# A top-k attention and quick-GELU kernel: from slot 25 on, all TensorE products as 64x64 quarters, in two halves across two PSUM banks, with units and loads in another order

## The chip, the cores and the metric

The kernel runs on one core of a Trainium2 chip. The metric is the device time of one execution in microseconds (us). The time of the kernel before is the median of three runs. One further execution was taken by the hardware profiler, and the profile and the trace come from it.

Engines are named as in the profile: PE (TensorE, the products), PEld (its weight loads), DVE (VectorE), ACT (ScalarE), POOL (GpSimd), SP (SyncE, which issues the DMAs).

## The reference

```python
# attention: q, k, v are (8, 8, 576, 64) float32; top_k = 32
scores = scale * np.matmul(q, k.transpose(0, 1, 3, 2))
kth = np.partition(scores, -top_k, axis=-1)[..., -top_k:-top_k + 1]
scores = np.where(scores >= kth, scores, -1000000000.0)
scores = scores - np.max(scores, axis=-1, keepdims=True)
attn = np.exp(scores)
attn = attn / (np.sum(attn, axis=-1, keepdims=True) + 1e-09)
attn_out = np.matmul(attn, v)                      # (B, H, S, D)
# bridge: x is (B*S, H*D) = (4608, 512)
h = x @ w_in                                       # w_in (512, 2048)
g = h * (1.0 / (1.0 + np.exp(-1.702 * h)))
return g @ w_out                                   # w_out (2048, 512)
```

Each row of scores keeps its 32 largest entries; the softmax over them weighs v. The result, heads side by side, goes through two matrix products with a quick GELU between them. All is float32.

## The kernel before, in words

**Slots.** The attention is cut into 144 slots, 18 for each of 8 batches (`slots`, from line 424). A slot is 128 query rows of two heads; the last 64 rows of a sequence (576 = 4 x 128 + 64) of two pairs of heads share a slot. For slot n:

- `scores(n)` (line 442) makes the scores on PE as 64x64 quarters into `score_banks` (tile s_ps); `copy_scores` (457) brings them to SBUF on ACT (sc).
- `pair_up` (466) makes the maximum and minimum of the two halves of a row on DVE; `topk` (486) finds the 32 largest by four rounds of MAX8 with MATCH_REPLACE8 between (tiles ranked and top). `find` (1172) runs slot m's rounds, with `pair_up(m + 1)` and `invert(m - 1)` (545: POOL some, DVE rden) among them.
- `bounds` (511) computes the threshold on POOL (cut, low); `mask` (526) and `exps` (534) make the masked exponentials on ACT (pr, den); `normalize` (559) scales them on POOL.
- `split` (595) copies pr apart in 16-bit halves on ACT (sc<-pr) and SP writes them to DRAM (rows); `turn_by_dma` (603) reads them back transposed (pt<-rows).
- `values_of_two` (675) multiplies two slots at once with v into two PSUM tiles (o): for the sequence's last 64 keys with v_e as quarters, for the others with v_l as 128x64 products (all 128 rows, half of the columns). `x_of_two` (703) copies them to xT on ACT.

**Blocks and units.** When all heads of 128 rows are there, they are a block (line 740). A block has four units of four pieces of 128 of the 2048 inner columns. For a unit: `hidden` (760) makes x @ w_in on PE (tile ph, 32 matmuls of 128x64, in one of the two buffers of `ps_t`, which o uses as well); `tanh` (782) takes tanh and a copy on ACT; `gate` (794) and `combine` (811) work on POOL and make the seven sums of a Strassen scheme on 2x2 blocks; `project` (864) multiplies them with w_out or its prepared sums into two PSUM banks (po0, po1; 28 matmuls of 128x64: seven products, two inner pieces, two column halves). After a block's fourth unit `leave_parts` (900) brings both banks to SBUF on ACT (raws<-po), POOL adds the products up (`merging`, by `merge_some`), and SP writes the rows out.

**Order.** Engines run their instructions in the order in which the kernel issues them. Up to slot 24 calls are collected and issued in a written-out order (ORDER, `issue_in_order`, 1358). From slot `COLLECTED` = 25 on `steady_pair(n)` (1281) issues two slots at a time. On PE a pair is: a projection, a hidden unit, s_ps of slot n+2, a hidden unit, a projection, s_ps of slot n+3, the values of slots n-3 and n-2. Behind the slots `last_units` (1347) finishes what is left. Every call passes through one recorder (line 131), so the profile has L131 for nearly all (L133 for what was collected).

**Loads.** `at(slot, ...)` (942) notes what falls due at a slot; `dues` (1150) hands it out. q and k of two heads are loaded (`load_both`, 371), split on ACT (`prepare_by_dma`, 375: halves), written to DRAM (qk_rows) and read back transposed (`turn` in it: qk_t<-qk_rows). FETCH (950) and READY (948) give the slots, relative to the batch's first, of the load and of the split.

## Time and profile before

| | |
|---|---|
| median of three runs | 1366.73 us |
| lowest and highest | 1366.28 and 1373.02 us |
| profiled execution: time | 1371.88 us |
| profiled execution: span of the program | 1370.1 us |
| granted TensorE clock, mean | 0.995 |
| DMA queue of the program | 526544 packets, 243.16 MB, 72.9% of 16 engines' span |
| PE instructions (products) | 22532, and as many weight loads |

How to read the profile's lines: a group line names the line of the kernel, engine and operation, then the tile written <- the tiles read, the shape, and xcount; behind it stand busy microseconds, the mean nanoseconds of one, and the engine's idle time before them with what ended it. The rows of the windows view give, for a stretch, each engine's busy time with its count of instructions, the granted clock, the DMA share and GB/s. The timeline merges like instructions that follow each other: start, time from the first start to the last end, what. Products of the code in float32 stand as two instructions each.

### The profile page before, as it was taken

To read this page: it belongs to the slowest core of one execution; us is meant where nothing else is said; L and a number is where in the kernel's file an instruction comes from. 1 tells how busy PE (TensorE), PEld (TensorE's weight loads), DVE (VectorE), ACT (ScalarE), POOL (GpSimd) and SP (SyncE) were. 2 spreads that over 40 slices of the span, in tenths; PEclk is the share of its full clock that TensorE was granted. 3 is DMA by queue.
4 is the path that set the end of the run, shared out by engine and by line. 5 is a ranking of instruction groups with operands and counts; after the bars stand their busy time and mean duration, and the time that the engine had idled before them with its cause. 6 is when DMAs were issued, how large, how long until landed. Compare 5 with 4: busy or idle time off the path is not lost.

```text
span 1370.1 us, 54342 instructions
## 1 busy us (share of the span) xinstructions
PE 1340.9 (98%) x22532; PEld 1202.3 (88%) x22532; DVE 1274.6 (93%) x3374; ACT 1166.2 (85%) x1936; POOL 978.4 (71%) x1782
## 2 busy tenths in 40 slices
PE   7899999999999999999999999999999999999998
PEld 5687588999989998999999999999998999999998
DVE  7999999999999999999999999999999999999912
ACT  6999898998889979898889888998988888888841
POOL 3888887777767776777777777777777777777770
PEclk9899999999999999999999999999999999999999
DMA  8443759677998767988899796988899767765540
GB/s 233 144 146 110 177 155 212 170 191 195 217 211 212 183 150 203 209 200 197 206 208 206 181 195 164 237 192 196 204 202 202 192 172 181 186 148 135 143 122 17
DMA packets 527223, 246.92 MB, mean 180 GB/s; under 512 B 458880, under 2 KB 505472, under 8 KB 526976
## 3 DMA queue, kind: packets, MB, share of 16 engines
q1 hardware_dynamic: 526544, 243.16, 72.9%
q8 instruction: 177, 2.90, 0.9%
q14 instruction: 70, 0.57, 0.1%
q10 hardware_dynamic: 432, 0.30, 0.1%
HBM read 46.01 MB, written 103.42 MB: 109 GB/s over the span
## 4 chain that ended last, share of the span: by engine, by line
PE 86%; DMA 4%; DVE 3%; ACT 3%; POOL 1%; SPq 1%; issue 1%; DVEq 0%; ACTq 0%; POOLq 0%
PE ph L131 31%; PE po L131 28%; PE o L131 10%; PE s_ps L131 9%; PE po L133 4%; DMA pt<-rows 2%; DVE ranked L133 2%; PE o L133 1%; DVE top L133 1%; PE s_ps L133 1%; SPq L131 1%; PE ph L133 1%; PE tp L133 1%; ACT sc L133 1%; DMA rows<-sc 1%
## 5 line engine op out<-in xcount | busy, mean ns | idle before, releaser
L131 DVE MAX8 top<-ranked 128x8 f32<-128x288 f32 (+1 forms) x952 | 526.7, 595 | 0.0
L131 PE MATMUL ph<-xT,win 128*64 128x128 f32 x8064 | 464.2, 273 | 0.0
L131 PEld LDWEIGHTS ph<-xT,win 128*64 128x64 f32 x8064 | 441.2, 137 | 25.9 <-issue 21.9
L131 DVE MATCH_REPLACE8 ranked<-top,ranked 128x288 f32<-128x288 f32 x714 | 382.0, 543 | 0.0
L131 ACT COPY sc<-pr 128x2304 uint16<-128x2304 uint16 x120 | 253.7, 2114 | 87.0 <-POOL pr L131 87.0
L131 POOL TENSOR_SCALAR pr<-pr,rden 128x576 f32<-128x576 f32 x240 | 177.3, 749 | 40.0 <-DVE rden L131 40.0
L131 PE MATMUL po<-wout,h 128*64 128x128 f32 x2000 | 194.2, 273 | 0.0
L131 PE MATMUL po<-raws,h 128*64 128x128 f32 x2000 | 194.2, 273 | 0.0
L131 ACT ACTIVATE pr<-sc,low 128x576 f32<-128x576 f32 x240 | 183.4, 770 | 0.2 <-POOL raws L131 0.2
L131 POOL TENSOR_SCALAR some<-den 128x2 f32<-128x2 f32 x120 | 26.7, 222 | 209.8 <-ACT pr L131 209.8
L131 ACT ACTIVATE sc<-sc,cut 128x576 f32<-128x576 f32 x240 | 174.1, 781 | 0.1
L131 DVE TENSOR_TENSOR ranked<-s_ps,sc 128x576 f32<-128x576 f32 x236 | 166.6, 747 | 4.3 <-ACT sc L131 4.3
L131 POOL TENSOR_TENSOR th<-th,h 128x512 f32<-128x512 f32 x123 | 157.7, 1282 | 10.3
L131 PE MATMUL po<-wout,th 128*64 128x128 f32 x2064 | 156.6, 273 | 0.0
L131 ACT COPY sc<-s_ps 128x576 f32<-128x576 f32 x234 | 138.0, 642 | 19.8 <-PE s_ps L131 9.7
L131 PE MATMUL s_ps<-qk_t 64*64 64x288 f32 x1872 | 140.5, 415 | 0.0
L131 PEld LDWEIGHTS po<-wout,h 128*64 128x64 f32 x2000 | 126.4, 137 | 0.0
L131 PEld LDWEIGHTS po<-raws,h 128*64 128x64 f32 x2000 | 126.4, 137 | 0.0
L131 PEld LDWEIGHTS po<-wout,th 128*64 128x64 f32 x2064 | 121.3, 137 | 0.0
L131 PE MATMUL o<-pt,v_l 128*64 128x128 f32 (+1 forms) x2144 | 120.7, 266 | 0.0
L131 PEld LDWEIGHTS o<-pt,v_l 128*64 128x64 f32 x2144 | 106.6, 137 | 9.9 <-issue 9.1
L131 POOL TENSOR_TENSOR h<-th 128x128 f32<-128x128 f32 x248 | 114.1, 460 | 0.3
(121 smaller groups left out, 2216.6 us busy)
## 6 DMA issues: line engine op xcount, KB each, us to landing
rows<-sc SPq DMA_DIRECT2D x134, 576.0 KB, 3.8
qk_rows<-halves SPq DMA_DIRECT2D x24, 576.0 KB, 5.2
out_dram<-raws SPq DMA_DIRECT2D x68, 128.0 KB, 3.6
raws<-in_moe_w_in_dram SPq DMA_DIRECT2D x16, 512.0 KB, 4.7
raws<-in_moe_w_out_dram SPq DMA_DIRECT2D x16, 512.0 KB, 3.7
qk_l<-in_q_dram SPq DMA_DIRECT2D x28, 256.0 KB, 4.2
qk_l<-in_k_dram SPq DMA_DIRECT2D x28, 256.0 KB, 4.4
v_l<-in_v_dram SPq DMA_DIRECT2D x4, 1024.0 KB, 7.5
```

The lines of the kernel that those rows point to most:

```text
L131: do(*args, **kwargs)
L133: self.engines.collected.append(lambda: do(*args, **kwargs))
```

## The change

From slot 25 on `quarter_pair` takes the place of `steady_pair`:

- Hidden units, projections and values are made of 64x64 quarters: 64 of the 128 rows of the contraction and 64 columns. Two units (or the two banks of a projection, or the two slots of the values) are made together. In a first half each quarter of the two PSUM banks takes one half of the rows (for hidden units and projections: rows 0 to 63 into one bank, rows 64 to 127 into the other); in the second half they change over, and a semaphore (`turned_over`), raised by the first half's last product, is waited for by the second half's first. The number of multiplications stays; the seventh product of the projection (s4 with b22) is split over both banks, so that 512 instead of 384 columns leave the second bank, and one more addition merges them.
- On PE a pair becomes: first half of two hidden units, first half of a projection, s_ps of slot n+2, second half of the hidden units, second half of that projection, first half of the next projection, s_ps of slot n+3, first half of the values, 8 matmuls of the projection's second half, second half of the values, the rest of the projection. At slot 25 one more projection is issued. `last_units` keeps its form for hidden units; its projections are in quarters where their block began so.
- Loads, splits and transposed reads of q and k move to other slots from the third pair of heads of batch 2 on.

```diff
...
@@ -225,7 +225,8 @@
     score_banks = pool("ps_s", 1, space=PSUM).tile([P, 2, 2, 512], F32, name="s_ps")
     ps_t = pool("ps_t", 2, space=PSUM)
     ps_p = pool("ps_p", 1, space=PSUM)
-    both_banks = [ps_p.tile([P, 512], F32, name=f"po{i}") for i in range(2)]
+    two_banks = lambda: [ps_p.tile([P, 512], F32, name=f"po{i}") for i in range(2)]
+    both_banks = two_banks()
     ident = const.tile([P, P], F32, name="ident")
     make_identity(tc.nc, ident[:])
@@ -397,6 +398,8 @@
         if b % 2 and hp > 1:
             at(b * PER + TURN, turn)
+        elif (b, hp) > (2, 1):
+            at(b * PER + READY[b % 2][hp] + 1, turn)
         else:
             turns.append(turn)
@@ -700,11 +703,76 @@
                 stop=(s, j) not in halves[k + 1 :],
             )
+    on_rows = lambda i: slice(i * TAIL, (i + 1) * TAIL)
+    turned_over = tc.alloc_semaphore("turned_over")
+    counted = [0]
+    def in_two_parts(homes, parts):
+        number = []
+        def part(n, first=0, last=None):
+            if n and not first:
+                nc.tensor.wait_ge(turned_over, number[0])
+            for home, at_, left, right, start, stop in parts[n][first:last]:
+                nc.tensor.matmul(homes[home][at_], lhsT=left, rhs=right, start=start, stop=stop)
+            if not n:
+                nc.tensor.drain(fusable=True).then_inc(turned_over, 1)
+                counted[0] += 1
+                number.append(counted[0])
+        return [lambda *some, n=n: part(n, *some) for n in range(2)]
+    two_turns = lambda: [ps_t.tile([P, 512], F32, name="tp") for _ in range(2)]
+    def values_in_quarters(held):
...
+        firsts, seconds = [], []
+        for k in range(0, len(of[0][1]), 2):
+            for o, ends, mains in of:
+                for r, j, cols, left, right in ends[k : k + 2]:
+                    firsts.append((o, j, r, cols, left, right))
+        own = {}
+        for o, j, r, *rest in firsts:
+            own[o, j] = r
+        for part, turned in ((firsts, 0), (seconds, 1)):
+            for k in range(len(of[0][2])):
+                for o, ends, mains in of:
+                    for j, cols, left, right in mains[k]:
+                        part.append((o, j, own[o, j] ^ turned, cols, left, right))
+        order = firsts + seconds
+        whose = [(o, j) for o, j, *rest in order]
+        steps = [
+            (
+                o, (on_rows(j), cols), left[on_rows(r)], right[on_rows(r)],
+                whose[k] not in whose[:k], whose[k] not in whose[k + 1 :],
+            )
+            for k, (o, j, r, cols, left, right) in enumerate(order)
+        ]
+        return homes, in_two_parts(homes, (steps[: len(firsts)], steps[len(firsts) :]))
     def x_of_two(held, o):
         for m, part in zip(held, o):
             b, t, hps = slots[m]
             x = xs[:, place_of(b, t), :, :]
+            part = part[:, 0:P]
             if t < NF:
                 nc.scalar.copy(out=x[:, hps[0], :], in_=part)
             else:
@@ -749,6 +817,7 @@
             if not self.whole:
                 self.left = [h * (FC // 2) + 2 * u + c for u in range(4) for h in range(2) for c in range(2)]
             self.done = 0
+            self.quarters = False
     ready = []
     to_gate, gated, to_project = [], [], []
@@ -779,6 +848,47 @@
         if not x.left:
             free.append(ready.pop(0).place)
+    quadrants = lambda a, b: ((a, 0, 0), (b, 1, 1), (a, 0, 1), (b, 1, 0))
+    def hidden_two():
+        if sum(len(x.left) for x in ready) < 2 * G:
+            return [lambda: hidden(ps_t), lambda: None]
+        units, homes = [], two_turns()
+        for _ in range(2):
+            x = ready[0]
+            fs, x.left = x.left[:G], x.left[G:]
+            units.append((fs, x))
+            if not x.left:
+                free.append(ready.pop(0).place)
+        parts = []
+        for turned in range(2):
+            part = []
+            for i in range(G):
+                for c in range(CC):
+                    for u, r, y in quadrants(turned, 1 - turned):
+                        fs, x = units[u]
+                        f = fs[i] * P + y * TAIL
+                        part.append(
+                            (
+                                u,
+                                (on_rows(y), slice(i * P, (i + 1) * P)),
+                                win[on_rows(r), c, f : f + TAIL],
+                                xs[on_rows(r), x.place, c, :],
+                                not turned and i == 0 and c == 0,
+                                turned == 1 and i == G - 1 and c == CC - 1,
+                            )
+                        )
+            parts.append(part)
+        first, second = in_two_parts(homes, parts)
+        def last():
+            second()
+            for ph, (fs, x) in zip(homes, units):
+                to_gate.append((ph[:], fs, x))
+        return first, last
     def tanh(aside):
         if to_gate:
@@ -861,8 +971,88 @@
         for _ in range(min(count, len(summing))):
             summing.pop(0)()
+    def leave_parts_of(x):
+        def leave_parts():
...
+            if x.quarters:
+                merging.append(add(o[:, 3, :], o[:, 3, :], o[:, 7, :]))
...
+    turned_last = [1]
+    def project_in_quarters():
+        if not to_project:
+            return [lambda: None, lambda *some: None]
+        x = to_project[0][3]
+        if not x.done:
+            x.quarters = True
+        if not x.quarters:
+            return [lambda: project(True), lambda *some: None]
+        g, sums, fs, x = to_project.pop(0)
+        a11, a12, a22, s1, s2, s3, s4 = sums
+        banks = (
+            ((1, a11, "b11"), (2, a12, "b21"), (0, s2, "t2"), (3, s4, "b22")),
+            ((0, a22, "t4"), (1, s1, "t1"), (2, s3, "t3"), (3, s4, "b22")),
+        )
+        parts = []
+        way = turned_last[0], 1 - turned_last[0]
+        for n, turned in enumerate(way):
+            part = []
+            for i in range(2):
+                for k in range(3 if turned else 4):
+                    for bank, r, y in quadrants(turned, 1 - turned):
+                        to, a, w = banks[bank][k]
+                        part.append(
+                            (
+                                bank,
+                                (on_rows(y), slice(to * P, (to + 1) * P)),
+                                a[on_rows(r), i, :],
+                                weight(w, fs[i])[on_rows(r), y, :],
+                                x.done == 0 and n == 0 and i == 0 and k == 0,
+                                x.done == FC - G and n == 1 and i == 1 and k == (2 if turned else 3),
+                            )
+                        )
+            parts.append(part)
+        turned_last[0] = way[1]
+        x.done += G
+        last = x.done == FC
+        first, second = in_two_parts(both_banks, parts)
+        def finish(*some):
+            second(*some)
+            if last and len(some) < 2:
+                leaving.append(leave_parts_of(x))
+        return first, finish
     def project(put_off_leaving=False):
+        if to_project[0][3].quarters:
+            for part in project_in_quarters():
+                part()
+            return leave_all()
         g, sums, fs, x = to_project.pop(0)
         if x.whole:
             for i, f in enumerate(fs):
@@ -897,30 +1087,8 @@
             for i in range(2):
                 nc.sync.dma_start(x.rows[:, i, :], ob[i * TAIL : (i + 1) * TAIL, :])
...
         if x.done == FC:
-            leaving.append(leave if x.whole else leave_parts)
+            leaving.append(leave if x.whole else leave_parts_of(x))
         if not put_off_leaving:
             leave_all()
@@ -947,7 +1115,6 @@
     READY = (-15, -11, -7, -3), (-17, -13, -9, -5)
     TURN = -3
-    FETCH = (-19, -13, -9, -5), (-19, -15, -11, -7)
     FETCH_1 = (-11, -6, -5, -4)
     VALUES = {(0, 1): 0, (2, 3): 2}, {(0, 1, 2, 3): 2}
     by_slot = dict(enumerate([2, 3, 3, 3, 3, 3, 3, 3, 3, 3, 3]))
@@ -966,9 +1133,12 @@
     for b in range(1, B):
         for hp in range(NP):
             if b > 1:
-                at(b * PER + FETCH[b % 2][hp], load_both, b, hp)
+                if (b, hp) < (2, 2):
+                    at(b * PER + (-19, -13)[hp], load_both, b, hp)
+                else:
+                    at(b * PER + READY[b % 2][hp] - 4, load_both, b, hp)
                 if (b, hp) != (2, 0):
-                    at(b * PER + READY[b % 2][hp], prepare_by_dma, b, hp)
+                    at(b * PER + READY[b % 2][hp] - 2 * ((b, hp) > (2, 1)), prepare_by_dma, b, hp)
             else:
                 at(b * PER + FETCH_1[hp], load_both, b, hp)
         for hps, n in VALUES[b % 2].items():
@@ -1344,6 +1514,79 @@
         if live(n + 1):
             bounds(n + 1)
+    def quarter_pair(n):
+        begin, prepare_some = dues(n)
+        if live(n - 1):
+            exponentials(n - 1)
+        combine()
+        merge_some(6 if n == COLLECTED + 2 else 3)
+        units = hidden_two()
+        units[0]()
+        leave_all()
+        first = project_in_quarters()
+        if n > COLLECTED:
+            first[0]()
+        prepare_some()
+        find(n, 8)
+        if live(n + 2):
+            scores(n + 2)
+        if n == COLLECTED:
+            first[0]()
+        units[1]()
+        first[1]()
+        if live(n - 1):
+            normalize(n - 1)
+            split(n - 1)
+        write_all()
+        gate()
+        begin(0)
+        if live(n - 1):
+            turn_by_dma(n - 1)
+        if live(n + 2):
+            copy_scores(n + 2)
+        if live(n):
+            bounds(n)
+        combine()
+        merge_some(4)
+        if live(n):
+            mask(n)
+            exps(n)
+        if n == COLLECTED:
+            leave_all()
+        tanh(True)
+        tanh(True)
+        prepare_some()
+        second = project_in_quarters()
+        second[0]()
+        find(n + 1, 8)
+        if live(n + 3):
+            scores(n + 3)
+        held = [m for m in (n - 3, n - 2) if live(m)]
+        o, values = values_in_quarters(held)
+        values[0]()
+        second[1](0, 8)
+        values[1]()
+        second[1](8)
+        if n == COLLECTED:
+            for part in project_in_quarters():
+                part()
+        if live(n):
+            normalize(n)
+            split(n)
+        write_all()
+        while turns:
+            turns.pop(0)()
+        begin(1)
+        if live(n):
+            turn_by_dma(n)
+        gate()
+        if live(n + 3):
+            copy_scores(n + 3)
+        x_of_two(held, o)
+        if live(n + 1):
+            bounds(n + 1)
     def last_units():
         hidden(ps_t)
@@ -1378,7 +1621,7 @@
             steady_pair(n)
         issue_in_order()
         for n in range(COLLECTED, N + 2, 2):
-            steady_pair(n)
+            quarter_pair(n)
         combine()
         while ready or to_gate or gated or to_combine or to_project:
             last_units()
```

More of the change, by code (lines that the diff above doesn't have):

```diff
@@ L130, in step @@
             if self.engines.collected is None:
-                do(*args, **kwargs)
+                return do(*args, **kwargs)
             else:
@@ L862, in sum_weights, with bring_out @@
             summing.pop(0)()
+    def leave_parts_of(x):
+        def leave_parts():
+            o = raws[:, 3, :].bitcast(F32).rearrange("p (r k) -> p r k", r=8)
+            for bank, count in enumerate((4, 4 if x.quarters else 3)):
+                nc.scalar.mul(
+                    out=o[:, 4 * bank : 4 * bank + count, :].rearrange("p r k -> p (r k)"),
+                    in_=both_banks[bank][:, 0 : count * P], mul=0.5 / RAISE**2,
+                )
+            add = lambda to, x, y: lambda engine: engine.tensor_tensor(out=to, in0=x, in1=y, op=ALU.add)
+            twice = lambda x: x.to_broadcast([P, 2, P])
+            merging.append(add(o[:, 0:3:2, :], o[:, 0:3:2, :], twice(o[:, 1:2, :])))
+            if x.quarters:
+                merging.append(add(o[:, 3, :], o[:, 3, :], o[:, 7, :]))
+            for to, by in ((6, 0), (0, 5), (3, 0)):
+                merging.append(add(o[:, to, :], o[:, to, :], o[:, by, :]))
+            merging.append(add(o[:, 4:6, :], o[:, 4:6, :], twice(o[:, 6:7, :])))
+            merging.append(lambda engine: writes.append(lambda: bring_out(o)))
+        def bring_out(o):
+            for y in range(2):
+                nc.sync.dma_start(
+                    x.rows[:, :, y * 2 * P : (y + 1) * 2 * P],
+                    o[y * TAIL : (y + 1) * TAIL, 2:6, :].rearrange("r (i h) k -> r i (h k)", i=2),
+                )
+        return leave_parts
@@ new lines @@
+    turned_last = [1]
[17 more added lines that the diff above has]
+            part = []
+            for i in range(2):
+                for k in range(3 if turned else 4):
[9 more added lines that the diff above has]
+                                x.done == FC - G and n == 1 and i == 1 and k == (2 if turned else 3),
+                            )
+                        )
+            parts.append(part)
[8 more added lines that the diff above has]
+        return first, finish
```

34 lines of the change are left out of this document (14 added, 20 removed).

## The prediction

> **What bounds the kernel now.** I read the page first, then the whole stretch that the change touches, then one pair of slots engine by engine.
>
> ```profile
> span 1370.1 us, 54342 instructions
> PE 1340.9 (98%) x22532; PEld 1202.3 (88%) x22532; DVE 1274.6 (93%) x3374; ACT 1166.2 (85%) x1936; POOL 978.4 (71%) x1782
> PE 86%; DMA 4%; DVE 3%; ACT 3%; POOL 1%; SPq 1%; issue 1%; DVEq 0%; ACTq 0%; POOLq 0%
> ```
>
> The chain that ended last is 86% TensorE. But the average hides a second engine. The reciprocal of a slot's denominators (tile rden) runs once in each slot, so its first and last start mark slots 25 to 143, and the windows view gives the busy time between them and in the tail behind them:
>
> ```profile
> L131 DVE RECIPROCAL rden<-some x119: 140/166/167, 265.2 to 1308.8; 128x2 f32<-128x2 f32 x119
> ```
>
> ```profile
> 265.00:1309.00 1044.00, 1040.85 (x18627) 953.61 (x18625) 1019.93 (x2698) 920.91 (x1494) 757.10 (x1446) 1.00 0.80 190
> 1309.00:1370.00 61.00, 55.15 (x1008) 54.22 (x1004) 9.45 (x25) 12.26 (x22) 21.74 (x36) 0.99 0.20 49
> ```
>
> Columns after the stretch and its length: PE, PEld, DVE, ACT, POOL. In the stretch with the slots PE idles 3.2 us and VectorE idles 24.1 us of 1044. VectorE's work is not changed, so **however much PE gets faster, this stretch cannot lose more than about 24 us**. The tail is PE alone.
>
> One pair of slots on PE (timeline; start, duration). Each float32 matmul of the code stands twice in the profile, so a hidden unit of 32 matmuls is x64; the po rows between the two shown run on to 711.69, and those between 714.84 and 717.90 are the second projection:
>
> ```profile
> 700.27 3.66 PE L131 MATMUL ph<-xT,win 128*64 128x128 f32 x64
> 703.86 1.20 PE L131 MATMUL s_ps<-qk_t 64*64 64x288 f32 x16
> 704.99 3.71 PE L131 MATMUL ph<-xT,win 128*64 128x128 f32 x64
> 708.54 0.61 PE L131 MATMUL po<-wout,th 128*64 128x128 f32 x8
> ...
> 711.69 1.20 PE L131 MATMUL s_ps<-qk_t 64*64 64x288 f32 x16
> 712.71 0.40 PE L131 MATMUL o<-pt,v_e 64*64 64x128 f32 x8
> 713.04 1.97 PE L131 MATMUL o<-pt,v_l 128*64 128x128 f32 x32
> 714.84 0.61 PE L131 MATMUL po<-wout,th 128*64 128x128 f32 x8
> ...
> 717.90 3.66 PE L131 MATMUL ph<-xT,win 128*64 128x128 f32 x64
> ```
>
> The pair takes 717.90 - 700.27 = **17.63 us on PE**. VectorE in the same time (timeline; the row of x4 at 711.71 holds the last two maxima of one slot and the first two of the next, so a slot goes from one such place to the next):
>
> ```profile
> 707.55 1.41 DVE L131 TENSOR_TENSOR ranked<-s_ps,sc 128x576 f32<-128x576 f32 x2
> 709.55 0.15 DVE L131 RECIPROCAL rden<-some 128x2 f32<-128x2 f32 x1
> 716.18 1.41 DVE L131 TENSOR_TENSOR ranked<-s_ps,sc 128x576 f32<-128x576 f32 x2
> 718.95 0.17 DVE L131 RECIPROCAL rden<-some 128x2 f32<-128x2 f32 x1 [0.69 <-POOL some L131]
> ```
>
> 716.18 - 707.55 = 8.63 us without a gap, so **17.26 us a pair is VectorE's floor**, 0.37 us under PE's 17.63. The next reciprocal comes 9.40 after the last one and shows who loses that time: PE is late with s_ps and the values, so ScalarE is late with its exponentials, GpSimd with "some", and VectorE waits.
>
> **The change, part by part.**
>
> *The form of the products.* A 128x64 product that used all rows becomes two of 64 rows, four of which run together. What one step costs is read from the rows above, with the length of one product:
>
> ```profile
> L131 PE MATMUL ph<-xT,win 128*64 128x128 f32 x8064 | 464.2, 273 | 0.0
> ```
>
> ```profile
> L131 PE MATMUL o<-pt,v_e x520: 216/269/320, 268.4 to 1295.9; 64*64 64x128 f32 x142, 64*64 64x64 f32 x32
> ```
>
> Old form: 64 instructions in 3.66, the last alone 0.27, so 31 steps of two in 3.39, **0.109 a step of two**. New form: v_e already has it (64*64, 128 columns, two PSUM tiles). Two steps of four take 0.40, less the last product 0.27, so 0.13 holds one step and the stagger of its four starts: 0.13 is the upper bound. s_ps, in the same form with 288 columns, makes four steps in 712.71 - 711.69 = 1.02, which is 0.113 for 128 columns with the entry. No row shows a reason for less than the old 0.109. I take **0.1095 a step of four**, the old one's, to which s_ps without its entry is nearest. Two products of the old form equal four quarters, so by themselves the products gain and lose nothing. What goes is the change of form around s_ps and v_e:
>
> - 703.86 to 704.99 is 1.13 for s_ps, where the second s_ps (v_e behind it in the same form) takes 1.02;
> - first hidden unit 3.59, second 3.55, against 32 steps x 0.109 = 3.49;
> - first projection 3.15 against 28 x 0.109 = 3.05; values 714.84 - 712.71 = 2.13 against 2 x 0.11 + 16 x 0.109 = 1.96.
>
> New pair: 64 + 56 + 18 = 138 steps x 0.1095 = 15.11, and two s_ps at 1.0, so **17.1 us against 17.63: 0.53 a pair less on PE**. That is below VectorE's 17.26, so the pair goes to 17.3. (The count of changes of form in the two programs' order: 250 before, 18 after, so the change does what it says.)
>
> *The semaphore between the halves.* Its increment rides on the last product of a first half. Waiting at the second half holds up everything behind it on PE. For hidden units and the first projection of a pair, between halves lie a projection part and s_ps (over 2 us); for the values only 8 matmuls, 4 x 0.11 = 0.44. The last product's result is there 0.27 after its start, 0.16 after its step: between 0 and 0.1, I take 0. In the tail two projections run their halves back to back: about 0.3 each.
>
> *Order on PE.* Both hidden first halves now follow the values closely: behind the last value product stand 16 matmuls of the projection (0.88) and then a step that needs both xT copies.
>
> ```profile
> 714.25 1.18 ACT L131 COPY sc<-s_ps 128x576 f32<-128x576 f32 x2 [0.84 <-PE o L131]
> 715.32 0.45 ACT L131 COPY xT<-o 128x128 f32<-128x128 f32 x2
> 715.63 1.47 ACT L131 ACTIVATE sc<-sc,cut 128x576 f32<-128x576 f32 x2
> 718.40 0.21 ACT L131 ACTIVATION_READ_ACCUMULATOR pr<-sc,low 128x1 f32 x1
> 718.50 0.98 ACT L131 ACTIVATE raws<-po 128x512 f32<-128x512 f32 x2
> ```
>
> Result 0.16 + copies 0.45 + two semaphores (0.1 each is my estimate) = 0.8 against 0.88: hidden, with nothing to spare. Every second pair a block's sums leave PSUM (raws<-po), which ScalarE does behind the exponentials: 719.48 - 715.63 = 3.85 after the masks begin, plus 0.1 for 128 more columns. Before, the next block's first projection came 8 us later; now it comes 3.5 (the hidden halves) after the projection's end. Values' end + 0.16 + 0.45 + 3.95 + 0.1 = 4.7 against 0.88 + 3.5 = 4.4: 0.3 in every second pair, up to 1 when the masks wait for VectorE. Bounds 0 to 0.5 a pair; I take 0.15, because PE then has 0.16 to spare against VectorE and a late PE hurts only past the reciprocal's slack. (Above, masks began at 715.63 and cost 0.77 there, so 714.86 would have cost none.) The one more GpSimd addition per block (about 0.46) lies in its idle time ("some" waits 207 us for ScalarE in this stretch, below).
>
> *Loads and transposes moved.* From batch 2 on q/k loads and their splitting come two slots earlier (one load in eight stays), and the transposing read comes three slots after the split instead of in the same pair of slots (the last two of odd batches stay). SyncE issues the same DMAs; they only move past rows/pt issues. Waits in the stretch:
>
> ```profile
> POOL some L131 <- ACT pr L131: 207.2, 119, 4.4
> DVE rden L131 <- POOL some L131: 18.6, 35, 3.7
> ACT xT L131 <- PE o L131: 15.3, 45, 0.5
> ACT sc L131 <- DMA rows<-sc: 6.7, 3, 3.9
> DVE ranked L131 <- ACT sc L131: 3.4, 3, 2.2
> PE o L131 <- DMA pt<-rows: 1.6, 2, 1.3
> ```
>
> DMA shows in few long waits (6.7 + 1.6 = 8.3 us in 5 places). I put that much of VectorE's 24.1 to DMA and leave it standing: bounds from all gone (-8) to doubled (+8).
>
> *The sum.* Stretch: 24.1 - 8.3 = 16 us of VectorE's idle time goes. This agrees with 59 pairs x (17.63 - 17.3 = 0.33) = 19, less the pairs that already run at VectorE's pace behind a long wait. Tail: three excursions of form at 0.3 less, two halves at 0.3 more: about 0.5 less. Together **-16.5 us** on the profiled execution (1371.9, span 1370.1), so 1355. That execution is 5 us above the median of the runs shown (1366.7); the same cut from the median gives **1350**, likely 1338 to 1360.
>
> **Rivals.**
>
> *A, slower: instructions come too slowly for steps of four.* Every product brings a weight load, and a step of four issues 8 instructions in 110 ns where the old step issued 4. This holds in every pair. For it: the stretch has never run so densely for long. Against it, the densest place:
>
> ```profile
> 536.17 0.41 PE L131 MATMUL o<-pt,v_e 64*64 64x64 f32 x16
> 536.51 2.08 PE L131 MATMUL o<-pt,v_l 128*64 128x64 f32 x64
> 538.42 0.61 PE L131 MATMUL po<-wout,th 128*64 128x128 f32 x8
> ```
>
> 80 products and 80 loads in 538.42 - 536.17 = 2.25 us, 14.1 ns each, against 13.7 within a step and (1104 + 64) / 17.26 = 14.8 as the new pair's mean. And v_e's 16 start within 0.41 - 0.22 = 0.19, 12 ns a product. But these rows are short and could be fed from a queue filled ahead. It decides from (17.63 - 2.0) / 138 = **113 ns a step**. If v_l's 1.91 / 64 = 30 ns a product (536.51 to 538.42) is a floor, a step takes 119: pair 18.4, +0.8 x 59 = +47, so **1413**. Instruction blocks are of a kind with it:
>
> ```profile
> q8 instruction: 177, 2.90, 0.9%
> rows<-sc SPq DMA_DIRECT2D x134, 576.0 KB, 3.8
> qk_l<-in_q_dram SPq DMA_DIRECT2D x28, 256.0 KB, 4.2
> ```
>
> 177 blocks for 45064 PE instructions are 255 each; a block now lasts 17.26 x 255 / 1168 = 3.8 us instead of 7.2. If only one is fetched at a time and lands like qk_l in 4.2, a pair takes 4.58 x 4.2 = 19.2: about +95, 1460.
>
> [...] Chance of A by any of these: 0.23.
>
> *B, no change: the new waits take the gap's place.* If the wait for raws<-po and the copies of xT come to 0.5 a pair or more (1 us in every second pair, and not absorbed), PE is at 17.6 again: **1363 to 1368**. For: both covers are worked out as thin. Against: VectorE's slack of 1.8 us at the reciprocal. Chance 0.12.
>
> *C, DMA:* the share is 0.80 already and pairs come 2% faster; if the long waits double and more, 8 us or 16 more stand against 16 gained: **1358 to 1368**, chance 0.06. If they vanish with the moved loads, 1342, within the forecast.
>
> **How the numbers follow.** Forecast 0.59, A 0.23, B 0.12, C 0.06. About 0.5% (7 us) is what a measurement of this kernel can tell from no change, so "faster" is under 1360: 0.57 of the forecast, 0.04 of B, 0.02 of C. "Same": 0.02, 0.08 and 0.03. "Slower": A's 0.23 and 0.01 of C. The range goes from 1338 (long waits gone, VectorE's floor reached) to 1413 (A at 119 ns, about half of A's chance); A's dearer forms are left out.
>
> **What would show it.** Right: steps of four 109 to 111 ns apart through the hidden units; no change of form around s_ps; pairs of 17.3 with VectorE idle under 10 us from slot 25 on; PE waiting for VectorE before s_ps. Wrong: steps over 113 ns or PE idle on issue (A); PE waiting for raws or xT over 0.5 a pair (B); more waiting for rows or pt than 8 us (C).

## The result, and the profile after

The changed kernel takes **1539.85 us** (median of four, 1538.94 to 1542.46) against 1368.47 for the kernel before (median of four). The ratio is 1.124, 95% interval 1.121 to 1.126: 12% slower, where 1350 had been forecast. The profiled execution took 1538.94 us at a granted clock of 0.99.

The page: span, busy time, the chain that ended last, and the DMA queue that brings instructions (count of blocks, MB, share).

```profile
span 1536.9 us, 88067 instructions
...
PE 1367.0 (89%) x39428; PEld 1254.9 (82%) x39428; DVE 1277.5 (83%) x3374; ACT 1178.5 (77%) x1936; POOL 989.5 (64%) x1813
...
q8 instruction: 309, 5.06, 1.4%
...
PE 75%; issue 9%; DMA 1%; ACT 0%; DVE 0%; DVEq 0%; ACTq 0%
```

TensorE's busy time grew by 26 us only, its share fell from 98% to 89%. VectorE's busy time is nearly the same (3 us more). "Issue" went from 1% to 9% of the chain: TensorE stood still for nothing that the profile shows. Instruction blocks went from 177 to 309; 5.06 MB in 309 blocks are 16 KB each.

The slots again by the first and last reciprocal, and the windows view of that stretch and the tail (columns: PE, PEld, DVE, ACT, POOL, then clock, DMA share, GB/s):

```profile
L131 DVE RECIPROCAL rden<-some x119: 143/166/168, 269.4 to 1472.6; 128x2 f32<-128x2 f32 x119
```

```profile
269.00:1473.00 1204.00, 1066.82 (x34996) 1008.19 (x34992) 1023.55 (x2698) 934.78 (x1497) 768.76 (x1479) 1.00 0.72 167
1473.00:1536.90 63.90, 55.70 (x1461) 52.90 (x1457) 8.70 (x25) 11.91 (x22) 22.21 (x38) 0.98 0.23 60
```

Of the 166.8 us by which the span grew, 160 are in this stretch (1204 against 1044). PE idles 137 us in it, before 3. A pair of slots takes (1472.6 - 269.4) / 59 = 20.4 us. The waits of the stretch (in total, times, longest) say behind what:

```profile
DVE rden L131 <- POOL some L131: 161.8, 85, 5.9
PEld po L131 <- issue: 98.7, 99, 2.8
...
PE po L131 <- issue: 74.8, 74, 2.6
...
PEld tp L131 <- issue: 71.1, 74, 3.3
...
PE tp L131 <- issue: 53.8, 61, 3.1
...
ACT sc L131 <- DMA rows<-sc: 16.6, 18, 2.2
```

Products and their weight loads stand still together, on issue and in every kind of unit; VectorE's wait is the end of the chain behind it. One pair on PE in the timeline:

```profile
702.61 0.27 PE L131 MATMUL po<-wout,th 64*64 64x128 f32 x1 [1.67 <-issue]
...
707.21 0.89 PE L131 MATMUL tp<-pt,v_l 64*64 64x128 f32 x24 [0.35 <-issue]
...
710.10 3.67 PE L131 MATMUL tp<-xT,win 64*64 64x128 f32 x128
...
715.76 0.27 PE L131 MATMUL po<-raws,h 64*64 64x128 f32 x1 [1.02 <-issue]
...
717.44 3.71 PE L131 MATMUL tp<-xT,win 64*64 64x128 f32 x128
```

The steps themselves are as priced: the hidden units' 128 products take 3.67, less 0.27 for the last, so 31 steps in 3.40, 0.110 each. What is lost lies between them, at places that have nothing to do with the program: in the middle of a projection, in the middle of the values. The trace has each transfer of the instruction queue; beside these pauses it reads (start and end of a block's transfer, then the moment at which PE goes on):

```
block 700.28 to 701.24    PE stands 700.66 to 702.61    1.37 after the block's end
block 704.89 to 705.84    PE stands 706.59 to 707.21    1.37
block 713.26 to 714.39    PE stands 714.46 to 715.76    1.36
block 735.01 to 735.97    PE stands 735.41 to 737.31    1.34
```

Over the stretch, 169 times more than 0.3 us lies between two starts on PE or PEld, 183 us in all. 151 of these, **177 us, end 1.15 to 2.0 us (median 1.40) after the end of a block's transfer**; in the kernel before it is 8 times, 2.8 us. (These count from start to start; PE's 137 us of idle time count from the end of the last product, 0.27 after its start.) Blocks come each 4.39 us on the mean (7.14 before), never closer than 3.25. Below, such pauses are called block pauses and the mean time from one block to the next is the block interval.

### The profile page after: what moved, and what is told of

Its sections match the earlier page's. It is cut to its first block, busy times and chain, and to the rows that moved or that the text cites. A ratio compares the mean times of both kernels' runs of the same rounds, so it can differ in the third digit from the quotient of the medians.

```text
span 1536.9 us, 88067 instructions
## 1 busy us (share of the span) xinstructions
PE 1367.0 (89%) x39428; PEld 1254.9 (82%) x39428; DVE 1277.5 (83%) x3374; ACT 1178.5 (77%) x1936; POOL 989.5 (64%) x1813
## 3 DMA queue, kind: packets, MB, share of 16 engines
q8 instruction: 309, 5.06, 1.4%
## 4 chain that ended last, share of the span: by engine, by line
PE 75%; issue 9%; DMA 1%; ACT 0%; DVE 0%; DVEq 0%; ACTq 0%
PE tp L131 38%; PE po L131 27%; PE s_ps L131 8%; PE ph L131 1%; DMA pt<-rows 1%; PE po L133 1%; PE ph L133 0%; PE o L133 0%; DMA rows<-sc 0%; ACT sc L133 0%; PE s_ps L133 0%; ACT pr L133 0%; DVE raws L131 0%; ACT raws L131 0%; DVEq L1655 0%
## 5 line engine op out<-in xcount | busy, mean ns | idle before, releaser
L131 PE MATMUL tp<-xT,win 64*64 64x128 f32 x15616 | 483.0, 271 | 40.0 <-issue 39.8
L131 PEld LDWEIGHTS tp<-xT,win 64*64 64x64 f32 x15616 | 456.9, 133 | 57.5 <-issue 53.4
L131 PE MATMUL po<-wout,th 64*64 64x128 f32 (+1 forms) x4048 | 358.1, 271 | 21.0 <-issue 20.8
L131 PE MATMUL po<-raws,h 64*64 64x128 f32 (+1 forms) x3984 | 357.5, 270 | 18.1 <-issue 18.1
L131 PE MATMUL po<-wout,h 64*64 64x128 f32 (+1 forms) x3984 | 296.8, 270 | 25.3 <-issue 25.2
L131 PEld LDWEIGHTS po<-wout,th 64*64 64x64 f32 (+1 forms) x4048 | 276.1, 133 | 30.2 <-issue 29.9
L131 PEld LDWEIGHTS po<-raws,h 64*64 64x64 f32 (+1 forms) x3984 | 275.7, 133 | 25.2 <-issue 25.0
L131 PE MATMUL po<-raws,th 64*64 64x128 f32 (+1 forms) x2024 | 245.1, 272 | 14.0 <-issue 12.5
L131 PEld LDWEIGHTS po<-wout,h 64*64 64x64 f32 (+1 forms) x3984 | 219.8, 133 | 28.5 <-issue 28.5
L131 DVE TENSOR_TENSOR ranked<-s_ps,sc 128x576 f32<-128x576 f32 x236 | 166.8, 748 | 18.5 <-ACT sc L131 18.3
L131 PEld LDWEIGHTS po<-raws,th 64*64 64x64 f32 (+1 forms) x2024 | 166.4, 133 | 19.3 <-issue 18.4
```

Of the source, the lines that this page charges most:

```text
L131: return do(*args, **kwargs)
```

## The experiments

Theories. **T1**: instructions arrive in blocks of 256 (2 x 39428 of PE in 309 blocks are 255 each), and the next is not there when a block has been used up; the quarters use them up too fast. **T2**: each instruction has a floor (20.4 us for 1168 of them would be 17.5 ns each). **T3**: the wait between the halves. **T4**: the new order, the moved loads, data that comes late.

| | what it is | PE instr. a pair | us | ratio to before [95%] |
|---|---|---|---|---|
| after | the change | 1168 | 1539.9 | 1.124 [1.121, 1.126] |
| e2 | no wait between halves | 1168 | 1550.2 | 1.128 [1.122, 1.135] |
| g2 | no rows written | 1168 | 1508.4 | 1.098 [1.087, 1.109] |
| g1 | no rows read back | 1168 | 1461.1 | 1.063 [1.053, 1.074] |
| e3 | neither | 1168 | 1412.2 | 1.028 [1.023, 1.033] |
| f3 | wide projections | 976 | 1413.5 | 1.031 [1.027, 1.035] |
| e4 | quarters in hidden units only | 880 | 1409.0 | 1.025 [1.023, 1.028] |
| f1 | all quarters wide | 656 | 1371.3 | 1.000 [0.997, 1.002] |
| f2 | f1 with the old loads | 656 | 1365.3 | 0.995 [0.993, 0.996] |
| e1 | old form in the new order | 624 | 1383.3 | 1.007 [1.005, 1.010] |
| e5 | e1 with the old loads | 624 | 1378.2 | 1.005 [1.003, 1.008] |

**e1: the new order without the new form.**

```diff
-                                win[on_rows(r), c, f : f + TAIL],
-                                xs[on_rows(r), x.place, c, :],
+                                    win[:, c, f : f + TAIL],
+                                    xs[:, x.place, c, :],
...
-        first, second = in_two_parts(homes, parts)
+        first, second = in_two_parts(homes, parts, False)
```

(False: without the semaphore; projections and values likewise.)

> The changed order of units, loads and transposes, but every product in the old form (128x64, all rows), and no semaphore between halves; 624 PE instructions a pair of slots instead of 1168. T1 (instruction blocks come too slowly for 1168 a pair): the time goes back to 1350 to 1372 us, and TensorE's idle time put down to issue falls from some 180 us to under 30. T4 (the new order, or the moved loads and transposes, cost the time): it stays at 1500 to 1540. T3 (the wait between halves costs it): like T1, 1350 to 1372, so this run does not tell T1 from T3.

1383.3 us: 157 of the changed kernel's loss are gone with the form, which leaves T4 at most the rest, and PE idles only 8 us of its stretch (1055 - 1047). But it is 0.7% slower than before, so the range was missed by 11 us: order and loads are not free.

**e5: e1, with the loads back.**

```diff
-                at(b * PER + READY[b % 2][hp] - 4, load_both, b, hp)
+                at(b * PER + FETCH[b % 2][hp], load_both, b, hp)
-        elif (b, hp) > (2, 1):
-            at(b * PER + READY[b % 2][hp] + 1, turn)
```

> As e1 (changed order of units, old form of products, no semaphore), with loads, splits and transposed reads of q and k back in the slots of the kernel before. If e1's 9 us come from the moved loads and transposes, this falls to 1366 to 1376 us; if from the order of units on TensorE, it stays at 1378 to 1390.

1378.2 us, at the lower edge of the second expectation (the order of units), and its interval overlaps that of e1. About 7 us of the order stay; what the loads take is settled by f1 and f2 below.

**e2: without the wait.**

```diff
-            if n and not first:
-                nc.tensor.wait_ge(turned_over, number[0])
...
-                        part.append((o, j, own[o, j] ^ turned, cols, left, right))
+                        part.append((o, j, own[o, j], cols, left, right))
```

> All quarters stay, but the second half keeps the sides of the first, so that nothing has to be waited for between halves: the semaphore is gone. (Half of the contraction's rows are counted twice and the other half is left out.) T1 (blocks): still 1530 to 1545 us, instructions and their blocks are the same in number. T3 (the wait between halves): back to about 1355. T2 (a floor for each instruction): as T1.

1550.2 us, 5 above the range of T1 (two runs, 1544 and 1556). Nothing comes back; T3 is out. The block pauses are there as before (159, 203 us).

**e4: a dose, hidden units alone.**

```diff
-                                a[on_rows(r), i, :],
-                                weight(w, fs[i])[on_rows(r), y, :],
+                                a[:, i, :],
+                                weight(w, fs[i])[:, y, :],
...
-        first, second = in_two_parts(both_banks, parts)
+        first, second = in_two_parts(both_banks, parts, False)
```

> A dose: the hidden units alone in quarters with their semaphore; projections and values in the old form, in the changed order. 880 PE instructions a pair, 3.44 blocks of 256. T1 (one block in about 4 us at best, some ahead): 3.44 x 4.4 = 15.1 us a pair is under 17.4, so on average the blocks suffice; only the quarter stretches of 3.5 us a block wait: 1365 to 1400 us. [...] T3 (each wait between halves costs a quarter of the loss): about 1410.

1409.0 us, 9 above the range of T1; T3's 1410 is met, but e2 has put T3 out. It is 26 above e1. Block pauses take only 10 us of its stretch (6 in e1). The rest is largely a cost that I had left out: quarters in hidden units and old form in projections change the form more often, 337 times between 269 and 1300 us against 230 in e1. The prediction has 0.53 us for the four changes of a pair, 0.13 each, so 107 of them make 14 us. The trace of e4 agrees: at a change the starts of two products lie 0.20 us apart, within a form 0.03 to 0.06 on the mean. Some 8 of the 26 us are left without a cause. Its time leaves T1 open; its pauses bear T1 out.

**e3: without the round trip of the exponentials.**

```diff
+        if n >= COLLECTED:
+            return
         rows = st[n]["rows"] = apart.tile([P, 2, 2 * S], U16, name="rows")
         nc.sync.dma_start(rows[:], halves)
...
+        if n >= COLLECTED:
+            st[n]["pt"] = kept[n % 2]
+            return
```

> The changed kernel without the round trip of the exponentials through DRAM from slot 25 on (rows are not written, pt is not read back; the values use two older pt tiles instead, so the attention of those slots is wrong and this traffic is left out). The same 1168 PE instructions a pair. T1, if a block is slow because it queues behind other transfers: blocks come more often than one in 4.39 us, gaps shrink, 1370 to 1470 us. T1, if a block takes a fixed time to fetch: still 1500 to 1540. T2 (a floor for each instruction): 1530 to 1540. T4 (data that comes late): about 1355 with gaps that end on data and not on issue.

1412.2 us, within the range for a block that queues behind other transfers. The same 1168 instructions a pair, and 128 us come back when the transfers go. The windows view of its stretch, DMA share 0.28 where the changed kernel has 0.72:

```profile
266.00:1345.00 1079.00, 1039.42 (x34995) 998.92 (x34990) 1018.13 (x2698) 925.28 (x1496) 767.45 (x1477) 1.00 0.28 59
```

Blocks come each 3.94 us (4.39 in the changed kernel), and 59 block pauses of 54 us are left. So a block's time depends on what else is moved; and T2, to which transfers are nothing, falls.

**f1: the same quarters with half of the instructions.** This is the run that could have acquitted the instructions. Form, halves, semaphore, order and loads stay; a product takes 256 columns where there were two with 128.

```diff
-                for c in range(CC):
+                for c in range(0, CC, 2):
...
-                                xs[on_rows(r), x.place, c, :],
+                                xs[on_rows(r), x.place, c : c + 2, :],
```

> The changed kernel (all quarters, halves, semaphore, order, loads and transposes as they are), but two quarter products with 128 columns become one with 256: as many columns pass TensorE, with 656 instead of 1168 PE instructions a pair. (The operands are no longer the right ones: sums of hidden units, projections and values are wrong.) T1 (instruction blocks): 2.56 blocks a pair, one in 6.7 us, so issue gaps behind blocks are gone and the time is that forecast for the change plus what the new order costs (e1 lost 9 us): 1345 to 1375 us. If the quarter form, the wait between halves or anything else of the change costs the time: 1500 to 1540.

1371.3 us: **168 us of the loss go with half of the instructions** (products and weight loads alike), as T1 expected. Its blocks, and its waits in the stretch:

```profile
q8 instruction: 185, 3.03, 0.9%
```

```profile
ACT sc L131 <- DMA rows<-sc: 15.9, 17, 4.3
...
PE tp L131 <- DMA pt<-rows: 10.3, 8, 2.8
...
ACT xT L131 <- PE tp L131: 8.2, 11, 2.8
PE po L131 <- ACT raws L131: 7.9, 20, 1.1
```

It also shows what the change would do if instructions cost nothing. VectorE sets the pace, as forecast; three slots of the timeline:

```profile
620.89 0.15 DVE L131 RECIPROCAL rden<-some 128x2 f32<-128x2 f32 x1
629.53 0.14 DVE L131 RECIPROCAL rden<-some 128x2 f32<-128x2 f32 x1
638.16 0.15 DVE L131 RECIPROCAL rden<-some 128x2 f32<-128x2 f32 x1
```

8.64 and 8.63 apart. But waits for rows and pt are 26 us where the kernel before had 8, and the gain is gone again.

**f2: f1 with the loads back** (the edit of e5 on f1).

> As f1 (all quarters, two products of 128 columns in one of 256, 656 PE instructions a pair), with loads, splits and transposed reads of q and k back in the slots of the kernel before. In f1 most slots kept VectorE's 8.63 us, but seven intervals of over 9.5 us from one slot to the next took up what was gained. If the moved loads make them (the DMA case): 1350 to 1362 us. If they come from the order of units or from chance: 1364 to 1376, as f1.

1365.3 us. That lies in the second expectation, not in that of the DMA case, and f2 still has eight intervals of over 9.5 us between slots, as many as f1 (counted over all 119 slots): the moved loads do not make them. But f1's and f2's intervals of the ratio do not meet: the moved loads cost about 6 us. The waits for DMA in its stretch are 15 us, not 26:

```profile
ACT sc L131 <- DMA rows<-sc: 8.0, 8, 3.0
PE tp L131 <- DMA pt<-rows: 7.4, 7, 2.4
```

It is the only run faster than the kernel before (0.5%), with sums that are not the reference's.

**f3: a dose without changes of form**: projections wide, the rest as changed.

```diff
-                for k in range(3 if turned else 4):
+                for k in (0, 2):
```

> A dose between f1 and the changed kernel: only the projections take 256 columns (their sums are wrong), hidden units and values stay quarters of 128 columns: 944 PE instructions a pair, 3.69 blocks, one in 4.7 us. T1 with a block in 4.4 us on the mean under load: 3.69 x 4.4 = 16.2 us a pair is under 17.3, so hardly any loss on the mean, but the hidden units' halves need a block in 3.5 us and one block of stock is soon used up: 1375 to 1420 us. A cost in proportion to the instructions (1371 + 288 / 512 of the 168 us between f1 and the changed kernel): 1465. T3: 1371, as f1.

The trace has 976 instructions a pair, not the 944 of the expectation (the projections keep 256 of their 448, since one product of the seven stays at 128 columns), so a cost in proportion would give 1371 + 320 / 512 x 168 = 1476. It is 1413.5 us, within T1's range and 63 under that. Of the 512 instructions a pair between f1 and the changed kernel the first 320 cost 42 us and the last 192 cost 126: a supply with a limit, not a price for each.

**m1, m2: the supply alone.** Only quarter products, 20 blocks in each stage, beside different transfers.

```python
def quarters(cols, blocks):
    for n in range(blocks * 256 // 16):
        for bank, r, y in ((0, 0, 0), (1, 1, 1), (0, 0, 1), (1, 1, 0)):
            nc.tensor.matmul(banks[bank][on(y), 0:cols], lhsT=w[on(r), y * 64 : y * 64 + 64],
                             rhs=w[on(r), 0:cols], start=n == 0, stop=n == blocks * 16 - 1)
...
for writes, reads, count in ((0, 0, 0), (1, 1, 20), (1, 0, 40), (0, 1, 40)):
    for cols in (64, 128):
```

> The disputed cost by itself: nothing but float32 quarter products on TensorE, 20 blocks of 256 PE instructions in each stage, with 64 and then with 128 columns, first without other transfers, then beside the kernel's own round trip (rows written, read back transposed), then beside the writes alone, then beside the transposing reads alone. (Nothing of the reference is computed.) With 128 columns TensorE needs a block each 3.5 us, with 64 about each 1.9. T1, one block at a time: without load both kinds get a block each 3.2 to 3.5 us (so 128 columns run without gaps and 64 columns starve), under load each 4 to 5 us, whatever the columns. T1 with a slow rate only in the kernel: 64 columns get blocks every 1.9 us without load. [...]

m1 does not answer: its transfers ran beside the stages that were to be quiet. m2 chains the stages one behind the other.

> The supply alone again, with its stages kept apart (in m1 the engines had been put in another order, and loads lay beside the stages meant to be quiet): float32 quarter products, 20 blocks of 256 PE instructions in each stage, with 64 and with 128 columns, beside nothing, beside writes and transposing reads in turn, beside writes alone, beside reads alone. (Nothing of the reference is computed.) T1, one block at a time in a fixed time plus what the load adds: with 64 columns a block each 3.3 to 3.5 us in quiet and 4 to 5.5 beside transfers, most beside the writes (share 1); with 128 columns no gaps in quiet, and gaps beside every load whose blocks take over 3.5 us. If a second block were fetched ahead: 64 columns in quiet a block each 2 us.

| m2, beside | DMA share | 64 columns: block interval, pauses | 128 columns |
|---|---|---|---|
| nothing | 0.02 | 3.67 us, 32 us | 3.61 us, none |
| writes and reads in turn | 0.57 to 0.60 | 3.84 us, 35 us | 3.87 us, 5 us |
| writes alone | 0.42 to 0.44 | 3.68 us, 33 us | 3.57 us, 0.4 us |
| transposing reads alone | 1.10 | 5.21 us, 46 us | 5.04 us, 29 us |

(The granted clock was 0.74 in the stage with reads and 64 columns, 0.96 to 1.00 in the others.) The timeline of the quiet stage with 64 columns is the clearest picture of T1; under it is the quiet stage with 128:

```profile
84.79 2.09 PE L70 MATMUL tp<-w 64*64 64x64 f32 x128 [1.36 <-issue]
88.52 2.09 PE L70 MATMUL tp<-w 64*64 64x64 f32 x128 [1.64 <-issue]
92.25 2.09 PE L70 MATMUL tp<-w 64*64 64x64 f32 x128 [1.64 <-issue]
...
163.74 16.58 PE L70 MATMUL tp<-w 64*64 64x128 f32 x589
```

128 products with their 128 weight loads are one block. They run in 2.09 us, 8 ns an instruction (T2 is out here as well), then PE stands 1.64 us, and the next block runs. With 128 columns a block lasts as long as the next takes, and nothing stands. I had expected 3.3 to 3.5 us in quiet and the longest interval beside the writes; it is 3.7, and the reads are what delays.

The trace also shows what the interval is made of. In the quiet stage with 64 columns the next block's transfer starts 1.15 us on the mean after PE has gone on, takes 1.16, and PE goes on 1.38 after its end: together 3.7. Beside the transposing reads only the first part grows, to 2.68; the transfer takes 1.05 and the last part 1.39. At the changed kernel's block pauses the three are 1.87 (from 1.03 to 4.11), 1.08 and 1.40, together 4.35. No transfer begins between the end of one and the moment at which PE goes on with it, at any of these pauses, and none sooner than 1.03 us after that moment: where PE starves, blocks are transferred strictly one at a time, each only after PE has gone on with the one before. That rules out the other expectation, a second block fetched ahead, by which 64 columns in quiet would have had a block each 2 us.

**g1, g2: which half of the round trip.** Each is one half of e3's edit.

> The changed kernel, rows of exponentials still written to DRAM, but not read back transposed from slot 25 on (the values use two older pt tiles; that traffic is left out). In the supply alone, blocks beside transposing reads came each 5.0 to 5.2 us, beside writes each 3.6 to 3.7, as in quiet. If it is the same in the kernel, this run recovers most of what the quiet kernel e3 did (1412): 1405 to 1435 us. If all transfers count alike by their share: about halfway, 1470 to 1490.

> The other half: from slot 25 on rows are not written, but two older rows tiles are read back transposed in each slot (the values of those slots are wrong; the writes are left out). If the transposing reads are what delays the blocks: 1490 to 1540 us, near the changed kernel. If all transfers count alike: 1470 to 1490. If it is the writes: 1405 to 1435.

Without the reads 1461.1, without the writes 1508.4: 79 and 31 us come back, 128 without both. Their stretches, one row each of the windows view:

```profile
264.00:1397.00 1133.00, 1052.80 (x35018) 1006.50 (x35010) 1021.26 (x2698) 930.47 (x1496) 769.03 (x1478) 1.00 0.43 117
```

```profile
261.00:1441.00 1180.00, 1065.33 (x34966) 1008.74 (x34960) 1021.97 (x2698) 932.68 (x1495) 767.00 (x1478) 1.00 0.61 112
```

The reads weigh more than the writes, but the writes are not nothing, as m2 alone would have had it: g1 lies between its two expectations, 1435 and 1470.

**The account.** The prediction's own stretch, without block pauses, was 1044 - 16 = 1028 us. With the block pauses that each trace shows, it gives every run:

| | block interval | block pauses | 1028 + pauses | stretch measured |
|---|---|---|---|---|
| after | 4.39 us | 177 us | 1205 | 1204 |
| e2 | 4.48 | 203 | 1231 | 1225 |
| g2 | 4.31 | 154 | 1182 | 1180 |
| g1 | 4.14 | 106 | 1134 | 1133 |
| e3 | 3.94 | 54 | 1082 | 1079 |
| f3 | 4.76 | 63 | 1091 | 1092 |
| f1 | 6.77 | 13 | 1041 | 1045 |
| f2 | 6.74 | 5 | 1033 | 1039 |

(e1, e4 and e5 change the form, so 1028 isn't theirs.) The pauses are taken from the same traces as the stretches, so this is an account and not a forecast; but nothing of size is left for another cause.

So no version that these runs point to beats the kernel before: fewer instructions in this form need products with more columns, which the data as it lies here offers to the projections at most, and f3, though its sums are not the right ones, shows 1413 for that. This is argued; no such version was run.

## Why the prediction was wrong

**The step that failed** is in rival A: "Instruction blocks are of a kind with it", with the chance "of A by any of these: 0.23" and "A's dearer forms are left out" of the range. The mechanism, its place and nearly its price were there: "If only one is fetched at a time and lands like qk_l in 4.2, a pair takes 4.58 x 4.2 = 19.2: about +95, 1460." Measured, a block comes each 4.39 us, and 1168 / 256 = 4.56 of them are 20.0 us; the pair takes 20.4, because some pairs have more than 1168 instructions: 274 blocks came in the 59 pairs, 4.64 each. The error is the chance, and behind it the evidence that I set against it: 160 instructions in 2.25 us. They show how fast instructions start, and 160 is less than a block. No burst shorter than what lies in stock says anything about the supply. In m2's stages with 64 columns the first pause comes only after 447 or 703 instructions; I should have asked for a run of several hundred at the new pace, and the kernel before has none: its blocks come each 7.14 us, never under 4.10. That 3.8 us lay outside everything that the trace held was the warning, and the sum put it at nothing.

A's other form, a floor for each product (30 ns, a step of 119), is shown by no run: the steps of the changed kernel were 0.110 apart, and in m2's quiet stage with 64 columns 128 products and their loads pass in 2.09 us, 16 ns a product.

By the prediction's other steps:

- *A step of four costs 0.1095:* right, 0.110 in the changed kernel. In f1, with 256 columns, 64 products in 3.66 us are as many columns in the same time.
- *Changes of form go, a pair comes to VectorE's 8.63 a slot:* right where instructions suffice (f1, f2). Between 270 and 1300 us 232 changes before, none after.
- *The semaphore, 0:* right within what e2 can show: without it the time did not fall.
- *xT's copies and raws leaving PSUM:* in f1 PE waits for raws in 20 places, 7.9 us, 0.13 a pair against 0.15 assumed. Rival B did not decide. The 0.1 for a semaphore had no row beside it; in the trace of before, ScalarE mostly starts 0.04 to 0.11 us after the end of the product that it waits for, and PE 0.05 to 0.11 after ScalarE's end, so 0.1 is the upper end of what is measured.
- *DMA waits of 8.3 us left standing, loads "only move":* wrong by some 6 to 18 us. f1 has 26 us of such waits, f2 with the old loads 15, and the two differ by 6 us in time. This is rival C, in a case hidden behind A; with f1 alone it would have made "no change" of a forecast of -16.
- *Order of units:* with the old form about +7 us (e5). The prediction had 0.15 a pair for the order, 9 us in 59 pairs, and let it vanish in PE's slack against VectorE, which the old form doesn't have. Whether these are the same microseconds is not shown.
- *The range's lower end:* with all long waits gone the sum gives 1350 - 8 = 1342, as rival C says; 1338 is 4 us lower than any term accounts for.
- *The chain of signs:* "PE idle on issue (A)" was named as what would show it wrong, and it is what the page showed first.

Not settled: why a block's transfer starts no sooner than 1.03 us after PE has gone on, and why PE needs another 1.4 after its end. Nor was tried what holds the start back beside transposing reads, their packets' number or their engines' time. The 4 us before slot 25 and the 3 us in the tail by which the changed kernel is also longer were not pursued; slot 25 begins between 261 and 270 us in all these runs.

## What to carry to other kernels

Where TensorE sets the pace, count its instructions and divide by 256: if a block of them is used up in less than the 4.4 us measured beside this kernel's transfers (3.7 in quiet, 5.2 beside transposing reads alone), the fetch sets the time, and instructions that pass at 8 ns each (m2) are dear. The other engines were not tried. Work cut into smaller products pays for it there; more columns in each product is the way back (168 us in f1). And a price taken from a short burst holds only as far as the stock behind it (447 or 703 instructions in m2).

## What the runs showed of the hardware

- Blocks of 256 PE instructions (128 float32 products and their weight loads) come at best 3.25 us apart (in the changed kernel), each 3.6 to 3.7 on the mean in quiet, 4.4 in the changed kernel, 5.0 to 5.2 beside transposing reads alone; PE goes on 1.4 us after a block's transfer ends.
- What other transfers lengthen is the time from PE going on to the start of the next block's transfer: 1.15 us in quiet, 1.87 at the changed kernel's block pauses, 2.68 beside transposing reads alone (64 columns). The transfer itself stays at 1.05 to 1.16.
- Writes of 576 KB one behind the other (DMA share 0.42) left the interval at 3.6 to 3.7 us, though in the kernel they had a part in it (g2).
- Four 64x64 products with 64 columns pass in (2.09 - 0.28) / 31 = 0.058 us, so TensorE's own pace would use up a block in under 1.9 us, half of what the fetch allows.
